# Two K loads of a grouped-query attention kernel, cut into a 96-row transfer and four 8-row transfers

## The chip, the cores and the metric

The kernel runs on one core of one Trainium2 chip. A core has five engines that matter here: TensorE (PE in the profile; its weight loads are the row PEld), VectorE (DVE), ScalarE (ACT), GpSimd (POOL) and SyncE (SP), which here does nothing but issue transfers. The transfers themselves are carried out by 16 DMA engines that belong to the core. The metric is the device time of one execution in microseconds (us); smaller is better. A measurement of this kernel is the median of a few executions.

## The reference

Sixteen batches, 32 query heads that share 8 key/value heads, 16 query positions, 2048 key positions, head size 128, all in bf16:

```python
B, Hq, Hkv, Sq, Sk, D = 16, 32, 8, 16, 2048, 128
k = jnp.repeat(k, Hq // Hkv, axis=1)
v = jnp.repeat(v, Hq // Hkv, axis=1)
scores = jnp.einsum("bhqd,bhkd->bhqk", q, k) * D ** -0.5
p = softmax(scores, axis=-1)
return jnp.einsum("bhqk,bhkd->bhqd", p, v)
```

K and V are 64 MiB each and are read once; q and the output are 2 MiB each. Four query heads of 16 positions share one K/V head, so each K/V head has 64 query rows.

## The kernel before, in words

The 128 K/V heads are taken in 64 pairs (index p, NP = 64) and the pairs in 32 groups of two (index Q, or n in the load function). One K load brings four heads: 2 MiB, as 128 partitions (rows) of 16 KiB that are contiguous in memory, into one of three buffers (`Kn`, NK = 3). One V load brings one pair: 1 MiB, each partition getting two runs of 4 KiB, into one of seven buffers (`Vb`, NV = 7). The last V load is cut in two along the key positions.

For each pair the steps are these. VectorE turns the K data around in 32x32 blocks (`kt`, L351, two instructions for each pair) into one of two buffers `KT`. TensorE forms the scores (S, L300 and L256). VectorE scales and negates them into SBUF, rearranged, and keeps the row minimum (L373). ScalarE takes the exponential with the row sum (L413). TensorE transposes the probabilities (PT, L312), ScalarE copies them out of PSUM (L423), TensorE multiplies them with V (PV, L330 and L336), and ScalarE, or VectorE for the last five pairs, scales the result by the reciprocal row sum (L436, L440, L394). GpSimd lays out the queries for the coming pairs (L174).

Every engine's program is written out by hand in a fixed order; semaphores tie the programs together. All transfers are issued by SP, in one order given by a loop over t: at an even t the K load t/2, then the V load of pair t-6, then the store of pair t-14, and every eighth step a load of q. SP issues them in that order and blocks at the first whose buffer is not free: a K load n waits until both transposes of both pairs of load n-3 are done (`sem_kt`), a V load until the product of pair p-7 is done (`sem_pv`), a store until its output tile is written.

Each transfer raises its semaphore by 16 in all, in sixteen increments of one. VectorE's wait for a K load stands ahead of the first transpose of a group and asks for all sixteen of each load that has used this buffer:

```python
if x == 0:
    dve.wait_ge(sem_k[Q % NK], 16 * (Q // NK + 1))
```

The change touches `load_k` in SP's program (L208) and this wait in `kt` in VectorE's program (the transposes are L351).

Of the kernel before, what the change touches and what calls it, by code (L numbers as in the profile page):

```python
# [11 lines left out]
NK = 3  # L12
# [11 lines left out]
LASTV = ((0, 12), (12, 16))  # L24
NFAST = 8
NLATE = 5


def both_heads(p, NP):
# [3 lines left out]
def bass_standalone__gqa_softmax__sampling_kernel(  # L33
# [28 lines left out]
    Kn = [sb(f"Kn{i}", [128, 4 * J * 128], BF16) for i in range(NK)]  # L62
# [19 lines left out]
    sem_k = [sem(f"sem_k{i}") for i in range(NK)]  # L82
# [19 lines left out]
    kf = k.rearrange("b h s d -> (b h s d)").rearrange("(n a x) -> n a x", n=NQD, a=128)  # L102
# [9 lines left out]
    def q_part(c, i):  # L112
        u = stage("Q", c, i)
        pe_prog.append(("QT", c, i, u))
        act_prog.append(("qe", c, i, u))

    def pv(p):
        pe_prog.append(("PV", p))
# [4 lines left out]
    def exp(p):  # L123
        act_prog.append(("exp", p))
# [11 lines left out]
    for p in range(NP - 2):  # L136
# [7 lines left out]
        if c + 1 < NQC and 2 <= i < 6:  # L144
            q_part(c + 1, i - 2)
    for p in range(NP - 2 - PVLAG, NP - NLATE):
        pv(p)
        norm(p)
    exp(NP - 2)
    exp(NP - 1)  # L150
    for p in range(NP - NLATE, NP - 3):
        pv(p)
# [11 lines left out]
    def o_ap(p):  # L164
        if p < NP - 4:
            return O_ps[:, 0:128]
        x = p - (NP - 4)
        return S_ps[:, 512 * x:512 * x + 128]

    def lay_q(eng, c):  # L170
        eng.wait_ge(sem_q[c % NQ], 16 * (c // NQ + 1))
        src = Qn[c % NQ][:, :, :].rearrange("p j (b x) -> p (j b) x", b=2)
        for r in range(4):
            eng.tensor_scalar(  # L174
                Q4[:, :, :, r, :].rearrange("p j b x -> p (j b) x"), src,
                mask[:, r:r + 1], None, op0=ALU.mult,
            ).then_inc(sem_q4, 1)

    with nc.Block() as block:

        @block.gpsimd
        def _(gp):
            gp.iota(iota_m[:, :, :], [[-8, 4], [-32, 4]], base=0, channel_multiplier=1).then_inc(sem_id, 1)
            gp.iota(iota_t[:, :], [[1, 128]], base=0, channel_multiplier=-1).then_inc(sem_id, 1)
            gp.wait_ge(sem_id, 2)
            gp.tensor_scalar(ident4[:, :], iota_t[:, :], 0.0, None, op0=ALU.is_equal).then_inc(sem_id, 1)
            gp.tensor_scalar(lo_m[:, :, :], iota_m[:, :, :], 0.0, None, op0=ALU.is_ge).then_inc(sem_id, 1)
            gp.tensor_scalar(hi_m[:, :, :], iota_m[:, :, :], 8.0, None, op0=ALU.is_lt).then_inc(sem_id, 1)
            gp.wait_ge(sem_id, 5)
            gp.tensor_tensor(lo_m[:, :, :], lo_m[:, :, :], hi_m[:, :, :], op=ALU.mult).then_inc(sem_id, 1)  # L190
            for x in range(2):
                gp.wait_ge(sem_id, 6 + x)
                a = lo_m[:, :, :] if x == 0 else hi_m[:, :, :]
                w = 2 >> x
                dst = hi_m[:, :, 0:2] if x == 0 else mask[:, :].unsqueeze(2)
                gp.tensor_tensor(dst, a[:, :, 0:w], a[:, :, w:2 * w], op=ALU.add).then_inc(sem_id, 1)
            gp.wait_ge(sem_id, 8)
            for c in range(1, NQC):
                gp.wait_ge(sem_st, last_q[c - 1, 3] + 1)
                lay_q(gp, c)  # L200

        @block.sync
        def _(sp):
            def load_k(n):
                s = n % NK
                if n >= NK:
                    sp.wait_ge(sem_kt, 4 * (n - NK) + 4)
                sp.dma_start(Kn[s][:, :], kf[n]).then_inc(sem_k[s], 16)  # L208

            def load_v(p):  # L210
                s = p % NV
                if p >= NV:
                    sp.wait_ge(sem_pv, p - NV + 1)
                if p < NP - 1:
                    dst = Vb[s][:, :, :, :].rearrange("a g j d -> a g (j d)")
                    sp.dma_start(dst, vf[:, 2 * p:2 * p + 2, :]).then_inc(sem_v[s], 16)
                    return
                for x, (lo, hi) in enumerate(LASTV):
                    dst = Vb[s][:, :, lo:hi, :].rearrange("a g j d -> a g (j d)")
                    src = vf[:, 2 * p:2 * p + 2, 128 * lo:128 * hi]  # L220
                    sp.dma_start(dst, src).then_inc(sem_vl[x], 16)

            def load_q(c):
                s = c % NQ
                if c >= NQ:
                    sp.wait_ge(sem_q4, 4 * (c - NQ + 1))
                src = qf[1024 * c:1024 * (c + 1), :].rearrange("(a j) d -> a j d", j=8)
                sp.dma_start(Qn[s][:, :, :], src).then_inc(sem_q[s], 16)

            def store(p):  # L230
                s = p % NO
                if p < NP - NLATE:
                    sp.wait_ge(sem_nm, p + 1)
                else:
                    sp.wait_ge(sem_nl, p - (NP - NLATE) + 1)
                sp.dma_start(of[128 * p:128 * (p + 1), :], Osb[s][:, :]).then_inc(sem_o[s], 16)

            for t in range(NP + SLAG + 1):
                for c in range(NQC):
                    if t == max(0, 8 * c - QLEAD):  # L240
                        load_q(c)
                if t < NP and t % 2 == 0:
                    load_k(t // 2)
                if 0 <= t - VLAG < NP:
                    load_v(t - VLAG)
                if 0 <= t - SLAG < NP:
                    store(t - SLAG)
            for s in range(NO):
                sp.wait_ge(sem_o[s], 16 * (NP // NO))
# [95 lines left out]
        @block.vector  # L345
        def _(dve):
            def kt(n, e):
                Q, x = divmod(n, 2)
                if x == 0:
                    dve.wait_ge(sem_k[Q % NK], 16 * (Q // NK + 1))  # L350
                dve.transpose(  # L351
                    KT[n % NKT][:, :].rearrange("p (t b g e a) -> p e g t b a", t=J // 4, b=2, g=4, e=2)[:, e],
                    Kn[Q % NK][:, :].bitcast(F32).rearrange(
                        "p (g x t e b c) -> p x e g t b c", g=4, x=2, e=2, b=2, c=32)[:, x, e],
                ).then_inc(sem_kt, 1)

            def recip(Q):
                dve.wait_ge(sem_exp, 2 * Q + 2)
                dve.reciprocal(rrec[:, 2 * Q:2 * Q + 2], rowsum[:, 2 * Q:2 * Q + 2]).then_inc(sem_rec, 1)  # L359

            dve.wait_ge(sem_id, 8)
            lay_q(dve, 0)
            for n in range(2):
                for e in range(2):
                    kt(n, e)
            for n in range(NP):
                Q, x = divmod(n, 2)
                dve.wait_ge(sem_s, n + 1)
                for y in range(2):
                    p = 2 * Q + y  # L370
                    if x == 0 and p >= NS:
                        dve.wait_ge(sem_exp, p - NS + 1)
                    dve.tensor_scalar(  # L373
                        Sneg[p % NS][:, 1024 * x:1024 * (x + 1)].rearrange("p (t a m) -> p t a m", t=4, m=8),
                        S_ps[:, 1024 * y:1024 * (y + 1)].rearrange("p (t m a) -> p t a m", t=4, m=8), -scale, None,
                        op0=ALU.mult, op1=ALU.min, accum_out=nhalf[:, x, p:p + 1],
                    ).then_inc(sem_max, 1)
                if x == 1:
                    dve.wait_ge(sem_max, 2 * n + 2)
                    pair = slice(2 * Q, 2 * Q + 2)  # L380
                    dve.tensor_tensor(nbias[:, pair], nhalf[:, 0, pair], nhalf[:, 1, pair], op=ALU.min).then_inc(sem_nb, 1)  # L381
                elif n >= 4:
                    recip(Q - 2)
                if n + 2 < NP:
                    for e in range(2):
                        kt(n + 2, e)
            recip(NQD - 2)
            for p in range(NP - NLATE, NP):
                if p == NP - 2:
                    recip(NQD - 1)  # L390
                dve.wait_ge(sem_rec, p // 2 + 1)
                dve.wait_ge(sem_o[p % NO], 16 * (p // NO))
                dve.wait_ge(sem_pv, p + 1)
                dve.tensor_scalar(Osb[p % NO][:, :], o_ap(p), rrec[:, p:p + 1], None, op0=ALU.mult).then_inc(sem_nl, 1)  # L394
# [75 lines left out]
```

## Time and profile before

| what | us |
|---|---|
| median of three executions | 342.99 |
| lowest and highest of them | 342.74, 343.7 |
| span of the profiled execution, first to last instruction | 340.7 |
| a time of the profiled execution beside its span | not recorded |
| median less that span | 2.3 |
| PE busy | 304.3 |
| DVE busy | 304.8 |
| ACT busy | 253.6 |
| POOL busy | 81.3 |
| DMA: mean rate, share of 16 engines' time on the transfer queue | 408 GB/s, 99.5% |
| 32 K loads of 2048 KB, median from issue to landing | 15.3 |
| 63 V loads of 1024 KB, median from issue to landing | 16.6 |

The first part of the profile's page gives busy time by engine over the whole span; the second cuts the span into 40 slices and gives each engine's busy share in tenths; the third gives the transfer queues, where q1 carries the kernel's own transfers and q8 and q14 carry instructions. The fourth follows the chain of work that ended last back from the end. The fifth and sixth group instructions and transfers by line. Beside the page, the trace holds the record of every transferred packet (start, duration, size, queue, but not the DMA engine) and the time of every increment of a load's semaphore; "landing" is the last of the sixteen.

### The profile page before, as it was taken

Reading aid. Unit: us, or ns where it says so; the run is one execution under the profiler, and the core shown is the slowest. Engines: PE = TensorE matmul, PEld = TensorE weight load, DVE = VectorE, ACT = ScalarE, POOL = GpSimd, SP = SyncE. Lnnn points to the kernel's source line nnn. Section 1 sums busy time; section 2 is a strip of 40 time slices with the busy share of each in tenths; the row PEclk is TensorE's granted clock in tenths of the full one; section 3 lists DMA queues with packets and bytes.
Section 4 is the critical chain, followed back from the end, with each engine's and each line's share of the span. In section 5 each row is a group of like instructions: output and inputs, shape, how many; then the busy total and the mean of one; then the engine's idle time right before and its main releaser. Section 6 shows DMA issues by size and latency. Waiting matters only on the chain.

```text
span 340.7 us, 7084 instructions
## 1 busy us (share of the span) xinstructions
PE 304.3 (89%) x3040; PEld 182.4 (54%) x2528; DVE 304.8 (89%) x457; ACT 253.6 (74%) x390; POOL 81.3 (24%) x40
## 2 busy tenths in 40 slices
PE   3466798999899998999989999999989999899987
PEld 3012355555655664566555556556645665555556
DVE  1879998999989997999989999899979999899952
ACT  3025776789777888778867897778887788678875
POOL 2840007500092004900075000920039000000000
PEclk9759999999999999999999999999999999999999
DMA  7999999999999999999999999999999999999993
GB/s 294 443 415 420 425 415 414 411 419 422 424 423 410 415 419 424 416 420 407 419 426 423 419 405 417 421 428 415 412 418 416 426 418 423 408 419 415 410 407 121
DMA packets 32688, 138.87 MB, mean 408 GB/s; under 512 B 10896, under 2 KB 11152, under 8 KB 28560
## 3 DMA queue, kind: packets, MB, share of 16 engines
q1 hardware_dynamic: 32656, 138.42, 99.5%
q8 instruction: 22, 0.36, 0.4%
q14 instruction: 10, 0.08, 0.1%
HBM read 136.31 MB, written 2.10 MB: 406 GB/s over the span
## 4 chain that ended last, share of the span: by engine, by line
PE 55%; DVE 28%; ACT 9%; issue 5%; DMA 2%; ACTq 0%; SPq 0%; DVEq 0%
PE O_ps L330 17%; DVE Sneg L373 17%; PE S_ps L300 14%; PE S_ps L256 12%; DVE KT L351 11%; PE ST_ps L312 8%; ACT P L413 4%; ACT QT L404 2%; DMA Kn<-in_k_dram 2%; PE ST_ps L278 2%; ACT PT L423 2%; ACT O L436 1%; PE S_ps L336 1%; PE O_ps L336 1%; DVE rrec L359 0%
## 5 line engine op out<-in xcount | busy, mean ns | idle before, releaser
L373 DVE TENSOR_SCALAR_CACHE_REDUCE Sneg<-S_ps 128x1024 f32<-128x1024 f32 x128 | 150.7, 1213 | 19.1 <-PE S_ps L256 18.9
L351 DVE STREAM_TRANSPOSE KT<-Kn 128x1024 f32<-128x1024 f32 x128 | 150.8, 1217 | 3.9 <-DMA Kn<-in_k_dram 3.9
L413 ACT ACTIVATE P<-Sneg,nbias 128x2048 bf16<-128x2048 f32 x64 | 128.2, 2004 | 16.1 <-DVE nbias L381 15.1
L300 PE MATMUL S_ps<-KT,QT 64*128 64x512 bf16 x512 | 103.5, 394 | 24.1 <-DVE Sneg L373 12.8
L174 POOL TENSOR_SCALAR Q<-Qn,mask 128x1024 bf16<-128x1024 bf16 x28 | 79.1, 2843 | 181.1 <-PE ST_ps L278 174.6
L256 PE MATMUL S_ps<-KT,QT 64*128 64x512 bf16 x512 | 103.1, 392 | 0.0
L330 PEld LDWEIGHTS O_ps<-Vb,PT 128*128 128x128 bf16 x672 | 62.4, 98 | 34.7 <-issue 28.0
L330 PE MATMUL O_ps<-Vb,PT 128*128 128x256 bf16 x672 | 80.7, 273 | 0.0
L423 ACT ACTIVATE PT<-ST_ps 128x512 f32<-128x512 f32 x128 | 69.3, 595 | 13.1 <-PE ST_ps L312 12.1
L300 PEld LDWEIGHTS S_ps<-KT,QT 64*128 64x128 bf16 x512 | 27.4, 94 | 93.7 <-issue 72.4
L312 PE MATMUL ST_ps<-ident,P 128*128 128x128 f32 x512 | 67.6, 275 | 4.1 <-ACT P L413 4.1
L436 ACT ACTIVATE O<-O_ps,rrec 64x128 bf16<-64x128 f32 x84 | 30.4, 362 | 46.2 <-PE O_ps L330 45.7
L312 PEld LDWEIGHTS ST_ps<-ident,P 128*128 128x128 f32 x512 | 56.9, 141 | 10.3 <-ACT P L413 7.8
L278 PE MATMUL ST_ps<-ident,Q 128*128 128x128 f32 x128 | 20.4, 291 | 5.2 <-DVE Q L174 5.2
L404 ACT ACTIVATE QT<-ST_ps 128x512 f32<-128x512 f32 x32 | 19.3, 604 | 5.1 <-PE ST_ps L278 5.1
L336 PEld LDWEIGHTS O_ps<-Vb,PT 128*64 128x64 bf16 x576 | 16.7, 110 | 11.5 <-issue 11.5
L336 PE MATMUL O_ps<-Vb,PT 128*64 128x128 bf16 x576 | 19.5, 221 | 0.6 <-ACT O L440 0.6
L278 PEld LDWEIGHTS ST_ps<-ident,Q 128*128 128x128 f32 x128 | 16.4, 152 | 5.2 <-issue 5.2
L413 ACT ACTIVATION_READ_ACCUMULATOR P<-Sneg,nbias 128x1 f32 x64 | 12.2, 191 | 0.0
L373 DVE DVE_READ_ACCUMULATOR Sneg<-S_ps 128x1 f32 x128 | 10.6, 83 | 0.0
L440 ACT ACTIVATE O<-O_ps,rrec 128x128 bf16<-128x128 f32 x17 | 6.0, 351 | 2.2 <-PE O_ps L336 2.2
L381 DVE TENSOR_TENSOR nbias<-nhalf 128x2 f32<-128x2 f32 x32 | 5.1, 160 | 1.1
(19 smaller groups left out, 20.1 us busy)
## 6 DMA issues: line engine op xcount, KB each, us to landing
Kn<-in_k_dram SPq DMA_DIRECT2D x32, 2048.0 KB, 15.3
Vb<-in_v_dram SPq DMA_DIRECT2D x63, 1024.0 KB, 16.6
Qn<-in_q_dram SPq DMA_DIRECT2D x8, 256.0 KB, 13.3
out_dram<-O SPq DMA_DIRECT2D x64, 32.0 KB, 16.1
Vb<-in_v_dram SPq DMA_DIRECT2D x1, 768.0 KB, 12.0
Vb<-in_v_dram SPq DMA_DIRECT2D x1, 256.0 KB, 12.3
```

The lines of the kernel that those rows point to most:

```text
L174: eng.tensor_scalar(Q4[:, :, :, r, :].rearrange("p j b x -> p (j b) x"), src, mask[:, r:r + 1], None, op0=ALU.mult,).then_inc(sem_q4, 1)
L256: return pe.add_instruction(mybir.InstMatmult(name=nc.get_next_instruction_name(), engine=mybir.EngineType.PE, ins=[pe.lower_ap(rhs), pe.l ...
L278: ins = pe.transpose(dst[:, 128 * j:128 * (j + 1)], src[:, 4 * x + j, b, :], ident4[:, :])
L300: ins = pe.matmul(s_ap, w, x, start=(acc == 0), stop=(acc == 3))
L312: ins = pe.transpose(dst[:, 128 * t:128 * (t + 1)], P[p % 2][:, 128 * x:128 * (x + 1)], ident4[:, :])
L330: ins = pe.matmul(O_ps[:, 0:256], pt[:, j // 2, j % 2, :], Vb[p % NV][:, :, j, :], start=(j == 0), stop=(j == J - 1),)
L336: ins = pe.matmul(o_ap(p)[64 * g:64 * (g + 1), :], pt[:, j // 2, j % 2, 64 * g:64 * (g + 1)], Vb[p % NV][:, g, j, :], start=(j == 0), stop ...
L351: dve.transpose(KT[n % NKT][:, :].rearrange("p (t b g e a) -> p e g t b a", t=J // 4, b=2, g=4, e=2)[:, e], Kn[Q % NK][:, :].bitcast(F32). ...
L373: dve.tensor_scalar(Sneg[p % NS][:, 1024 * x:1024 * (x + 1)].rearrange("p (t a m) -> p t a m", t=4, m=8), S_ps[:, 1024 * y:1024 * (y + 1)] ...
L413: act.activation(P[p % 2][:, :].bitcast(BF16), Sneg[p % NS][:, :], ACT.Exp, bias=nbias[:, p:p + 1], scale=-1.0, accum_out=rowsum[:, p:p + ...
L423: act.activation(PT[p % NPT][:, 4 * h:4 * (h + 1), :].rearrange("p t q -> p (t q)"), stage_ap(u), ACT.Copy,).then_inc(sem_ev, 1)
L436: ins = act.activation(Osb[p % NO][rows, :], O_ps[rows, 128 * g:128 * (g + 1)], ACT.Copy, scale=rrec[rows, p:p + 1])
```

## The change

Two of the 32 K loads, number 14 and number 22, are issued as five transfers instead of one. First come four transfers of eight partitions each: partitions 96, 100, ..., 124, then 97, 101, ..., 125, then 98, ..., 126, then 99, ..., 127. The fifth brings partitions 0 to 95. Together they bring the same 128 rows of 16 KiB into the same buffer. Each of the five adds 16 to the buffer's semaphore, so VectorE's wait counts 80 for a cut load and 16 for any other that has used this buffer. Nothing else changes.

```diff
+KCUT = (14, 22)
+KROWS = 96
...
                 if n >= NK:
                     sp.wait_ge(sem_kt, 4 * (n - NK) + 4)
-                sp.dma_start(Kn[s][:, :], kf[n]).then_inc(sem_k[s], 16)
+                if n not in KCUT:
+                    sp.dma_start(Kn[s][:, :], kf[n]).then_inc(sem_k[s], 16)
+                    return
+                for a in range(KROWS, KROWS + 4):
+                    sp.dma_start(Kn[s][a::4, :], kf[n, a::4]).then_inc(sem_k[s], 16)
+                sp.dma_start(Kn[s][:KROWS, :], kf[n, :KROWS]).then_inc(sem_k[s], 16)
...
                 if x == 0:
-                    dve.wait_ge(sem_k[Q % NK], 16 * (Q // NK + 1))
+                    dve.wait_ge(sem_k[Q % NK], sum(80 if m in KCUT else 16 for m in range(Q % NK, Q + 1, NK)))
```

## The prediction

> **What bounds the kernel now.** I read the page first (busy shares, the slices, the transfer queues), then the waits, then the chain that ended last, and then the K loads one by one.
>
> ```profile
> PE 304.3 (89%) x3040; PEld 182.4 (54%) x2528; DVE 304.8 (89%) x457; ACT 253.6 (74%) x390; POOL 81.3 (24%) x40
> DMA  7999999999999999999999999999999999999993
> DMA packets 32688, 138.87 MB, mean 408 GB/s; under 512 B 10896, under 2 KB 11152, under 8 KB 28560
> q1 hardware_dynamic: 32656, 138.42, 99.5%
> q8 instruction: 22, 0.36, 0.4%
> q14 instruction: 10, 0.08, 0.1%
> PE 55%; DVE 28%; ACT 9%; issue 5%; DMA 2%; ACTq 0%; SPq 0%; DVEq 0%
> ```
>
> Two things run at their limit together: the 16 DMA engines are busy from the first slice to the last but one, and DVE and PE at 89%. The chain belongs to PE and DVE, with DMA 2%. So no transfer is waited for after the first, which the list of waits says too:
>
> ```profile
> DVE KT L351 <- DMA Kn<-in_k_dram: 3.9, 1, 3.9
> SPq L208 <- DVE KT L351: 123.5, 24, 10.5
> ```
>
> The only wait of DVE for K is at the start. SP waits 123.5 us for buffers: transfers are queued far ahead. How far is seen by load: 7.8 us from issue to landing at the least, 20.2 at the most. The answers for K28, K31 and for DVE's use of K31 (the window from 315.9) are
>
> ```profile
> L208 SPq DMA_DIRECT2D Kn<-in_k_dram x1: 328/328/328, 264.8 to 264.8; - x1
> DMA to landing us min/median/max: 20.2/20.2/20.2
> ...
> L208 SPq DMA_DIRECT2D Kn<-in_k_dram x1: 1220/1220/1220, 295.8 to 295.8; - x1
> DMA to landing us min/median/max: 19.9/19.9/19.9
> ...
> L351 DVE STREAM_TRANSPOSE KT<-Kn x2: 1201/1212/1222, 316.2 to 317.4; 128x1024 f32<-128x1024 f32 x2
> ```
>
> K31 is issued at 295.76, lands 19.85 later at 315.61 and is transposed from 316.24: a margin of 0.62 us. Done for all loads by the trace's increments and DVE's starts, the margin is 13.7 us at K3, 8.8 at K14, 8.1 at K15, 4.7 at K22, 4.0 at K23, 3.4 at K26, 2.6 at K27, 1.06 at K28, 2.3 at K29, 1.55 at K30, 0.62 at K31. It falls because DMA is the slower of the two: from K14 to K15 loads land 10.14 us apart, while eight pairs (four loads) take the chain 39.8 us (its PV pieces at 124.39 and 164.21). The last V load's two parts are issued at 324.03 and 324.5 and land 12.0 and 12.3 later, about 1.2 us before PE needs them. From 295 to 325.6 DVE runs without a gap in the chain. So an earlier landing gains nothing in this execution, and a later one costs all that goes beyond 0.6 us at K31 or 1.06 at K28.
>
> The sixteen increments of one load say how unequal the DMA engines are. In K4 they all come within 0.57 us. In K31 they come, from the first, at 0, 0.09, 0.33, 0.41, 0.51, 0.91, 2.77, 2.95, 3.07, 3.17, 3.28, 3.34, 3.76, 4.35, 4.39 and 4.58 us; in K28 at 0, 0.04, 0.28, 0.33, 0.44, 0.82, 2.80, 2.81, 2.86, 2.91, 2.94, 3.00, 3.02, 3.13, 3.29, 3.34. One increment jumps by about 1.5 us after each of the 16 KiB packets of q8 (the first starts at 41.7 us and takes 1.11): an instruction fetch delays the one DMA engine that it falls on, and as none is ever idle the lag stays until the end. Six are hardly touched, ten are late. A load lands when the latest has.
>
> **The change part by part.** Profiled execution: span 340.7, some 2.3 below the median of 342.99; I add the difference below to the median and take what lies around the span as unchanged.
>
> *Rows moved.* 32,688 packets less 28,560 under 8 KB leaves 4,128: the 4,096 rows of 16 KiB of K and 32 of the two instruction queues. So a row is one packet, never cut, and an 8-row transfer can occupy at most eight DMA engines, a 128-row one gives each of 16 eight rows, a 96-row one six. If the four small transfers go to the same eight, these get 4 + 6 = 10 rows of a cut load and the others 6. A row of K takes 0.611 us (median of the 4,096 packets, 608 to 1,586 ns between its ends, the latter in the cold first load). Two rows more in each of two loads: 4 x 0.611 = 2.44 us more on eight engines, 2.44 less on the other eight. Four more closing increments of 9 ns in each load add 0.07. Bounds: 0, if the four transfers alternate between two sets of eight; 36.7, if all 32 rows of a cut load went to one engine (38 rows in place of 8, 30 x 0.611 in each of two loads). I take 2.44, nearest to the row we have: every 128-row load splits evenly. The upper end would give 379 us and stays outside the range with the chance that I leave there.
>
> [...] No trace here shows an 8-row transfer, nor which of the engines are the late ones.
>
> *What of that is felt.* At K14 and K22 themselves the margins of 8.8 and 4.7 cover 1.22 and 2.44. The lag stays, though. At K28, if the eight that get more are the eight least late (up to 2.81), the landing moves from 3.34 to 2.81 + 2.44 = 5.25: 1.91 later, 0.85 beyond the margin. If the latest is among them, 2.44 - 1.06 = 1.38. At K31, best case 2.95 + 2.44 = 5.39 against 4.58: 0.81 later, 0.19 beyond the margin; worst 2.44 - 0.62 = 1.82. A shift at K28 makes DVE late and gives K31 as much margin back, so they don't add: +0.85 in the best case, +1.82 in the worst. Nine times in ten, eight drawn of sixteen hold one of the three latest of K31 (4.35 and more), which gives +1.6 to +1.8. Ten are late and only six early, so no choice of eight avoids a late one. The last V load (lag 4.9, margin 1.2) asks for less than K31. I take +1.6, toward the worst.
>
> *The wait.* VectorE's wait counts to 80 instead of 16. One semaphore wait as before, nothing else behind it; 0. It asks for five transfers where one was asked for, and the last of them lands as above. Behind it on DVE stand the transposes of two pairs, and behind these PE's scores, up to now covered by K14's and K22's margins.
>
> *SP.* Eight more issues. A K issue takes 0.33 us, a V issue 0.44 (0.33 to 5.5 when it is held up). 4 x 0.33 = 1.3 us in each cut load, before the 96 rows and the V load, store and q load behind them. Landing is 14.2 us after issue at K14 and 18.3 at K22, all of it queue, so the engines don't run dry: 0. Were that cover gone, 1.3 us would be waited for at each. Below: nothing is saved, as no issue is removed.
>
> *Bytes.* The same; 0. Rows stay contiguous pieces of 16 KiB, and every fourth row of memory is read by each small transfer, close to each other in time.
>
> Sum: 342.99 + 1.6 = 344.6, own range +0.85 to +1.82, so 343.8 to 344.8.
>
> **The rivals.**
>
> *Two writers for the same partitions' memory.* Today partitions 96 to 127 are written by the engines that always write them, each row at 27.2 GB/s (from 4 KiB packets of 0.159 us and 16 KiB of 0.611: 12,288 B in 0.452 us). With the change other engines write them while their usual writers write theirs. If the way into a group of partitions carries only what one engine does, both run at half rate during the four rows: 4 x 0.611 = 2.44 more for both, per load. Then the eight lag 2 x (1.22 + 2.44) = 7.3, and at K31 7.3 - 0.62 = 6.7: 349.7; if the 96 rows are split so that two engines meet as well, more. For it: slope and size of the packets allow a limit at either end. Against: no packet after the first loads shows such a slowdown, but there is no case of two in this trace either. [...] Chance 0.26.
>
> *Hidden, or not done.* The small transfers alternate over the engines, or timed executions have more margin at K28 and K31 than the profiled one: 343.0. Against it: the profile's margin of 0.62 is what the trace shows. Chance 0.14.
>
> *SP held up.* Some issues take 2.8 us (K25) and up to 5.5. Four at 2.8 are 11.2 us, against K22's margin of 4.7: 6.5 felt, 349.5. It decides only when the queue of 18.3 us has run out. Chance 0.06.
>
> *Faster.* The engines that get more rows are the six early ones and two whose lag is there only in the profile. Then the eight stand at 0.91 + 2.44 = 3.35 at most, the others at 4.58 - 2.44, and K31 lands 4.58 - 3.35 = 1.2 earlier. The time falls by what executions wait for loads there, at most 1.2: 341.8. It decides only if the timed executions wait more than 1 us for K, where the profiled one waits for none after the first. Chance 0.06.
>
> **How the numbers follow.** A measurement of this kernel can tell 0.3%, 1.03 us. The forecast has 0.48, of which 0.10 lies under +1.03. Faster: 0.06. Within 0.3%: 0.14 + 0.10 = 0.24. Slower: 0.38 + 0.26 + 0.06 = 0.70. The range goes from 342.8, below the hidden case, to 349.8, above the two at 349.5 and 349.7; outside lie the faster case and the larger prices of two writers.
>
> **What would show it.** Right: 16 KiB packets of K14 and K22 still 0.61 us; the increments after K14 moved by 1.22 us up for eight and down for eight, twice that after K22; waits of DVE on Kn of 1 to 2 us in all, at K28 to K31; SP's issues of 0.33. Two writers: packets of 1.2 us at K14 and K22. Hidden: no wait of DVE on Kn after the first. Wrong altogether: a spread of the increments at K31 that is smaller than 4.58, or DVE and PE groups that change in busy time.

## The result, and the profile after

The changed kernel takes 361.82 us (median of four executions, 360.73 to 361.99) against 342.87 for the kernel before in the same comparison (341.87 to 343.7): a ratio of 1.0555, 95% interval 1.0534 to 1.0576. It is 19 us slower, where 1.6 had been forecast, and outside the range given (342.8 to 349.8). The sign was right, the size was not.

The page of the changed kernel: its span, the DMA rows of the forty slices (8.97 us each here), and the chain by engine and line.

```profile
span 358.9 us, 7092 instructions
DMA  8999999999999999999999999999999999999992
GB/s 317 431 410 420 417 423 423 415 412 410 423 418 429 422 348 223 380 420 411 414 420 419 421 423 315 210 253 420 415 418 421 417 419 417 418 419 418 393 389 87
PE 44%; DMA 21%; DVE 21%; ACT 7%; issue 4%; SPq 3%; ACTq 0%; DVEq 0%
DMA Kn<-in_k_dram 21%; PE O_ps L337 14%; DVE Sneg L380 12%; PE S_ps L307 11%; PE S_ps L263 10%; DVE KT L358 8%; PE ST_ps L319 6%; ACT P L420 3%; ACT QT L411 2%; SPq L223 1%; PE ST_ps L285 1%; ACT O L443 1%; ACT PT L430 1%; PE S_ps L343 1%; PE O_ps L343 1%
```

The same rate in the kernel before, in slices of 8.52 us:

```profile
GB/s 294 443 415 420 425 415 414 411 419 422 424 423 410 415 419 424 416 420 407 419 426 423 419 405 417 421 428 415 412 418 416 426 418 423 408 419 415 410 407 121
```

Two holes stand in the GB/s row of the changed kernel, in its 15th to 17th and 25th to 27th slice: there the rate falls from about 420 to 223 and 210 GB/s. The DMA row above it shows no hole: the DMA engines are as busy as ever (99.3% of their time on the transfer queue, 99.5 before). They move half as much in the same busy time. The chain, which had 2% of DMA, now has 21%, all of it on K loads.

The waits and the K rows of the changed kernel, first DVE's total wait for K with its count and its longest, then the issues with their durations in ns (lowest, median, highest):

```profile
DVE KT L358 <- DMA Kn<-in_k_dram: 20.2, 6, 12.1
...
L211 SPq DMA_DIRECT2D Kn<-in_k_dram x30: 327/432/2211, 1.2 to 314.5; - x30
L214 SPq DMA_DIRECT2D Kn<-in_k_dram x8: 623/623/1288, 125.3 to 213.1; - x8
L215 SPq DMA_DIRECT2D Kn<-in_k_dram x2: 438/438/438, 128.1 to 213.8; - x2
```

DVE waited 3.9 us for K before; now it is 20.2, one wait alone 12.1. The two holes by windows (the last two columns are the share of the DMA engines' time and GB/s), before:

```profile
132.00:142.00 10.00, 8.53 (x97) 4.82 (x79) 8.51 (x13) 7.92 (x13) 9.28 (x4) 1.00 1.01 415
220.00:240.00 20.00, 19.50 (x214) 12.01 (x180) 19.76 (x30) 16.48 (x25) 3.66 (x2) 1.00 1.03 420
```

and after:

```profile
132.00:142.00 10.00, 8.79 (x101) 5.25 (x83) 8.47 (x13) 7.90 (x12) 8.54 (x4) 1.00 1.03 223
220.00:240.00 20.00, 12.86 (x132) 7.71 (x108) 9.43 (x14) 11.64 (x18) 4.85 (x2) 0.96 1.03 222
```

In the first window compute does the same as before (DVE 8.51 and 8.47): K14's margin of 8.8 us covers it. In the second, DVE falls from 19.76 to 9.43. The packet records say what halved the rate: from 132.0 to 145.5 us and from 219.75 to 240.75 nearly every packet in flight, 14 to 18 of them at a time, takes about twice its time (a K row 1.17 us in place of 0.611, a V row 0.32 in place of 0.159). Outside the two stretches hardly a packet is slow (51 of the K and V rows after the first 20 us take over 1.3 times the usual). Added up over the packets and divided by 16 engines, the loss is 6.7 us in the first stretch and 10.4 in the second. Landings follow: K15 lands 7.6 us later than before (156.47 against 148.91), K23 19.3 later, K31 18.7 later. Less the margin of 0.62 at K31 that is 18.1; the span has grown by 18.2.

The increments of K14's semaphore also show how an 8-row transfer is carried out: there are 52 for the five transfers, 16 for the 96 rows and nine for each small one. Four come 0.00, 0.72, 1.39 and 2.06 us after the first of them, at SP's four issues; the other 48 from 6.2 us on. The page counts 64 packets under 512 B more than before (10,960 against 10,896), eight for each of the eight small transfers, where a load of 128 rows has sixteen increments, as many as there are DMA engines. Read so, eight engines take part in a small transfer with an increment each; 48 of the 80 that the wait asks for come this way, and the four at SP's issues bring the other 32, eight each.

### The profile page after: what moved, and what is told of

Read it like the earlier page. It is cut to its first block, busy times and chain, and to the rows that moved or that the text cites. A ratio compares the mean times of both kernels' runs of the same rounds, so it can differ in the third digit from the quotient of the medians.

```text
span 358.9 us, 7092 instructions
## 1 busy us (share of the span) xinstructions
PE 307.8 (86%) x3040; PEld 183.4 (51%) x2528; DVE 305.5 (85%) x457; ACT 254.0 (71%) x390; POOL 81.4 (23%) x40
## 2 busy tenths in 40 slices
DMA packets 32752, 138.87 MB, mean 387 GB/s; under 512 B 10960, under 2 KB 11216, under 8 KB 28624
## 3 DMA queue, kind: packets, MB, share of 16 engines
q1 hardware_dynamic: 32720, 138.42, 99.3%
## 4 chain that ended last, share of the span: by engine, by line
PE 44%; DMA 21%; DVE 21%; ACT 7%; issue 4%; SPq 3%; ACTq 0%; DVEq 0%
DMA Kn<-in_k_dram 21%; PE O_ps L337 14%; DVE Sneg L380 12%; PE S_ps L307 11%; PE S_ps L263 10%; DVE KT L358 8%; PE ST_ps L319 6%; ACT P L420 3%; ACT QT L411 2%; SPq L223 1%; PE ST_ps L285 1%; ACT O L443 1%; ACT PT L430 1%; PE S_ps L343 1%; PE O_ps L343 1%
## 5 line engine op out<-in xcount | busy, mean ns | idle before, releaser
L358 DVE STREAM_TRANSPOSE KT<-Kn 128x1024 f32<-128x1024 f32 x128 | 150.9, 1218 | 20.2 <-DMA Kn<-in_k_dram 20.2
L307 PE MATMUL S_ps<-KT,QT 64*128 64x512 bf16 x512 | 105.2, 400 | 38.8 <-DVE Sneg L380 27.7
L263 PE MATMUL S_ps<-KT,QT 64*128 64x512 bf16 x512 | 104.8, 397 | 0.0
L411 ACT ACTIVATE QT<-ST_ps 128x512 f32<-128x512 f32 x32 | 19.3, 603 | 5.1 <-PE ST_ps L285 5.1
## 6 DMA issues: line engine op xcount, KB each, us to landing
Kn<-in_k_dram SPq DMA_DIRECT2D x30, 2048.0 KB, 18.9
```

What stands on the lines that cost most here:

```text
L263: return pe.add_instruction(mybir.InstMatmult(name=nc.get_next_instruction_name(), engine=mybir.EngineType.PE, ins=[pe.lower_ap(rhs), pe.l ...
L307: ins = pe.matmul(s_ap, w, x, start=(acc == 0), stop=(acc == 3))
L358: dve.transpose(KT[n % NKT][:, :].rearrange("p (t b g e a) -> p e g t b a", t=J // 4, b=2, g=4, e=2)[:, e], Kn[Q % NK][:, :].bitcast(F32). ...
```

## The experiments

What was known by now: rows take twice their time while a cut load is under way. The theory, A: when two DMA engines write into partitions of the same group, they share what one can carry, so the rival of the prediction, but with the 96 rows at fault as well. No trace names the engine of a packet, so which engines write which partitions is an assumption of this theory throughout. Its rivals: B, only the four small transfers do it; C, only the lag of the extra rows; and a fourth, the mere number of transfers, issues and increments.

**The parts by themselves.** A kernel of loads only, one kind after the other on an idle queue (the helpers, one for each kind, are left out here):

```diff
+plan = [(rows_128, 1), (rows_96, 1), (rows_128, 1), (rows_64, 1), (rows_32, 1),
+        (small_high, 4), (small_low, 4), (small_next, 4), (five, 5), (rows_96, 1), (five, 5)]
+for n, (what, c) in enumerate(plan):
+    what(n, sems[n])
+    done(sems[n], c)
```

> This kernel computes nothing: it only issues loads of K rows on an idle queue, each waiting for the one before, and stores the last. Order: 128 rows, rows 0 to 95, 128 rows, rows 0 to 63, rows 96 to 127, the four small transfers of the change, the same four on partitions 0 to 31 (every fourth), four of eight neighbouring rows, all five of the change, rows 0 to 95 again, all five again. Theory A (two DMA engines that write rows of the same group of partitions share one engine's rate, and the 96 rows are dealt out six to an engine without regard to who usually writes them): packets of 0.61 us in the 128 rows, of 1.2 us in the 96, 64 and 32 rows, 0.61 in both four-apart sets (each set of eight rows has one writer per group when it is alone), up to 2.4 in neighbouring rows; the five together are slower than the 96 rows and the four small ones are alone. Theory B (only the small transfers are at fault): the 96 rows alone have packets of 0.61 and land in 6/8 of the time of 128. Theory C (no sharing, only the extra lag that was predicted): packets of 0.61 throughout, the five land 2 x 0.61 = 1.2 us later than the 128 rows.

Its transfers by size, with the median from issue to landing in us:

```profile
A<-in_k_dram SPq DMA_DIRECT2D x4, 1536.0 KB, 9.1
A<-in_k_dram SPq DMA_DIRECT2D x2, 2048.0 KB, 7.8
A<-in_k_dram SPq DMA_DIRECT2D x1, 1024.0 KB, 7.3
A<-in_k_dram SPq DMA_DIRECT2D x1, 512.0 KB, 4.4
```

96 rows take longer than 128 (9.1 against 7.8), and 64 rows nearly as long (7.3). The packets agree: a median of 0.611 us in the 128 rows, 1.08 in the 96, 1.27 in the 64, 1.08 in the 32. The four small transfers alone have medians of 0.79 (96 to 127) and 0.69 (0 to 31), 41% of them at 0.61, though theory A had written 0.61 for both; four of neighbouring rows, 2.09. All five of the change land 13.6 and 14.0 us after the first issue, some 6.1 more than one load of 128. B and C fall: 96 rows are slow with nobody else there (1.08 us a row).

**Three ways to cut the same two loads.** Without small transfers; with the small ones on partitions 0 to 31; and along the row, in five transfers of the same bytes:

```diff
 # two_parts
+sp.dma_start(Kn[s][KROWS:, :], kf[n, KROWS:]).then_inc(sem_k[s], 16)
 sp.dma_start(Kn[s][:KROWS, :], kf[n, :KROWS]).then_inc(sem_k[s], 16)
 # low_rows
+for a in range(4):
+    sp.dma_start(Kn[s][a:32:4, :], kf[n, a:32:4]).then_inc(sem_k[s], 16)
+sp.dma_start(Kn[s][32:, :], kf[n, 32:]).then_inc(sem_k[s], 16)
 # columns
+for a in range(4):
+    x = slice(512 * a, 512 * (a + 1))
+    sp.dma_start(Kn[s][:, x], kf[n][:, x]).then_inc(sem_k[s], 16)
+sp.dma_start(Kn[s][:, 2048:], kf[n][:, 2048:]).then_inc(sem_k[s], 16)
```

> Both loads in two transfers, rows 96 to 127 in one and rows 0 to 95 in the other, so no 8-row transfer and no engine with more rows than another. Theory A: the 96 rows still meet, so most of the 18.9 us stays: 355 to 365 us. Theory B (the small transfers are at fault): 343 to 345. Theory C (lag by extra rows): 343.

> [...] Theory A: the 96 rows still meet: 352 to 362 us. Theory B: the small transfers now write where they always did, so only the lag is left: 343.5 to 345. Theory C: as the change without sharing, 344.6, which the change itself has already missed.

> The same two loads in five transfers with the same bytes in each, but cut along the row: four of 128 rows of 1 KiB and one of 128 rows of 12 KiB. [...] Theories A, B and C: no meeting and no lag, 342.5 to 343.5 us. A fourth theory (the number of transfers, SP's issues or the wait for five increments is at fault): about 362.

Against before (343.0): two parts 358.37, ratio 1.0426 (1.0375 to 1.0477); small ones on the low rows 358.7, 1.0475 (1.0416 to 1.0534); columns 342.9, 1.0002 (0.9988 to 1.0016). The slices of the two-part kernel:

```profile
GB/s 315 424 417 421 417 428 414 417 413 412 421 421 424 424 346 201 365 416 413 415 421 420 422 422 360 192 267 419 421 421 420 422 419 415 414 417 420 409 400 98
```

and of the columns:

```profile
GB/s 289 441 417 420 425 418 411 409 420 425 419 417 418 411 422 410 424 410 413 419 422 432 412 408 417 410 425 422 408 419 415 430 412 425 409 419 416 410 406 120
```

Cutting a load in five along the row costs nothing. Cutting it into 96 and 32 rows costs 15 of the 19 us, with no 8-row transfer in sight. So the number of issues, the wait for 80 increments and the bytes are cleared, as the prediction had them at 0.

**One cut at a time.**

```diff
-KCUT = (14, 22)
+KCUT = (14,)   # only14;  (22,) only22;  (4,) only4
```

> Only load 14 is cut, as the change cuts it. In the changed kernel's trace loads land 7.6 us later from K15 on and 19.3 later from K23 on. If each cut costs what its own meeting of writers costs, whatever went before: 7.6 less the margin of 0.62 at K31, 350 us. If the two cost the same and the trace's split is chance: 9.5 less 0.6, 352. If the lag alone did it (predicted): 343 to 344.

> Only load 22 is cut. If the second cut costs more because the engines are further apart by then through their own fetches of instructions: 11.7 less 0.6, 354 us. If it costs more because the first cut has spread them: about 350, as with load 14. The sum of this and the run with load 14 alone, counted from before, should come to 18.9 plus 0.6 if the cuts are independent.

Load 14 alone: 349.74 against 342.54, ratio 1.0203 (1.0180 to 1.0226), 7.2 us. Load 22 alone: 350.85, 1.0241 (1.0221 to 1.0261), 8.3; of the two figures written for it, "about 350" holds. Together 15.5, less than the 19 of both. Each run alone has K31's margin of 0.6 taken off, both together only once, so independent cuts would add up to 0.6 less than 19 (the expectation adds the 0.6 where it has to be taken off). The 2.8 us that are missing then say that a second cut is dearer after a first. Counted from the packets (quarters of a us in which most of those in flight take over 1.3 times the usual), the time at half rate is 14.0 us with load 14 alone, 16.5 with load 22 alone, and 13.5 and 21.25 in the changed kernel. What differs ahead of them is how far the sixteen engines have come apart: the increments of the load before the cut come within 2.2, 3.4, 2.1 and 6.2 us. That it is the spread was read from the runs afterwards; load 4, where the spread is smallest, puts it to a test:

> Only load 4 is cut, where the DMA engines are still in step: in the trace of before the sixteen increments of K4 come within 0.6 us, those of K13 within 2.0 and those of K21 within 3.3. Load 14 alone cost 2.03%, load 22 alone 2.41%. If the half rate lasts as long as any engine still has a row to write in another's partitions, and so longer the further apart the engines are: 5.5 to 6.5 us, what the five cost in a stretch without compute (6.5 to 7.4 there) less the margin, 348.2 to 349.2. If the cost is the same wherever the cut is: 349.7 to 351. If an early cut is made up for, as its margin of 13 us is large: 343 to 345.

346.75 against 342.92, ratio 1.0108 (1.0076 to 1.0140): 3.8 us. The direction is as the theory says, but none of the three ranges written holds: 346.75 lies below 348.2. The 6.5 to 7.4 us that it was taken from (the five between whole loads without compute, below) were a poor measure. The time at half rate is 10.75 us at a spread of about 0.6 (K3, 0.8 in this execution). Its slices fall to 291 and 295 GB/s, not to 223 and 210:

```profile
GB/s 304 442 411 291 295 419 418 426 420 412 413 417 422 427 413 419 409 421 419 427 420 413 416 415 421 423 427 409 412 419 423 424 421 412 419 415 418 411 409 129
```

So 10.75, 14.0, 16.5 and 21.25 us of half rate stand beside spreads of 0.8, 2.2, 3.4 and 6.2: about 1.9 us more for each us of spread (10.5 over 5.4). Counted in the same way, the kernel with two parts has 13.75 and 17.25 us at spreads of 1.9 and 3.5, a little above this line. The kernel with the low rows has 13.75 and 16.25 us at 2.0 and 5.1, and for the last of these the line gives 18.9. So with the same cut the half rate lasts longer where the engines are further apart, but that the spread is what lengthens it is not shown. An early cut is not made up for by a margin of 13 us: the DMA engines' share is 1.01 and 1.02 in the windows from 26 to 38 and from 40 to 50 us, with no pause in which to catch up, and K31 lands 4.4 us late (320.03 against 315.61).

**Extra rows, with all loads whole.** Here nothing is cut. Four times, four transfers of eight rows of 7 KiB are loaded in addition into a tile that nobody reads. Only the partitions differ: 0 to 31, 96 to 127, 32 to 63 and 4 to 35, in the order of the expectations.

```diff
+if n in (14, 17, 20, 23):
+    ...  # wait until the extra rows of the batch before have landed
+    for a in range(P0, P0 + 4):
+        sp.dma_start(Xt[a:P0 + 32:4, :], kf[n, a:P0 + 32:4, 0:3584]).then_inc(sem_x, 16)
 sp.dma_start(Kn[s][:, :], kf[n]).then_inc(sem_k[s], 16)
```

> All loads uncut. In addition, ahead of loads 14, 17, 20 and 23, four transfers each of eight rows of 7 KiB (partitions 0, 4, ..., 28 and so on) into a tile that nobody reads: bytes that the kernel before does not move. [...] So eight engines get 16 rows of about 0.27 us more, 4.35 us of lag, and nobody meets. By the prediction's step on what a lag costs: 2.8 us (the eight least late get it; from K28: 2.81 + 4.35 - 3.34 - 1.06) to 3.7 (the latest are among them; from K31: 4.35 - 0.62), so 345.8 to 346.7. If a lag is made up for somewhere: 343 to 344.

> [...] No 96-row transfer. Theory A (two writers of a group of partitions share one engine's rate): both are slowed while they meet, so 4.35 us come on top for the eight and as much for their partners: 348 to 351. If the small transfers' place does not matter and the 96 rows did all of it: as with partitions 0 to 31, 345.8 to 346.7.

> The extra 7 KiB rows go to partitions 32 to 63. If what counts is who writes a group of partitions in the uncut loads, and partitions 32 to 63 belong to the same eight engines as 0 to 31 in the same order, this is the run with partitions 0 to 31 over again: 345.5 to 346.5. If any place but 0 to 31 meets: 350 to 356.

> [...] If the meeting is between an engine and the usual writer of the partitions, the same eight engines now carry the lag, the slower foreign rows and the slower own rows: 4.35 + 4.35 + 4.35 at a fair share, 13 less 0.6, so 355, and up to 364 at double that price. If only partitions 64 to 127 make trouble: 345.5 to 346.5.

| partitions | us | before | ratio (95%) |
|---|---|---|---|
| 0 to 31 | 345.9 | 342.54 | 1.0094 (1.0075 to 1.0113) |
| 32 to 63 | 346.16 | 342.93 | 1.0095 (1.0070 to 1.0120) |
| 96 to 127 | 354.99 | 342.54 | 1.0361 (1.0336 to 1.0385) |
| 4 to 35 | 355.25 | 342.93 | 1.0358 (1.0317 to 1.0400) |

The first two cost what a pure lag would: 3.4 and 3.2 us for an estimated 4.35 us of rows on eight engines, inside the 2.8 to 3.7 that the prediction's step gives. Partitions 32 to 63 behave as 0 to 31 (346.16 and 345.9 us; DVE's waits for K are 7.9 and 7.3 us, against 17.1 with 96 to 127 and 16.3 with 4 to 35). The last two rows cost 9 us more for the same bytes, again through eight engines for each transfer (144 increments for sixteen transfers). The run with 96 to 127 lies above both ranges written for it (348 to 351 at most). Shifting by four partitions is enough (1.0358 against 1.0094). All four runs read their rows with the same step in memory, so the reading does not make the difference; where the rows are written does. The author's reading, with the same eight engines in all four runs, is that what matters is whether an engine writes into partitions that another engine writes in the whole loads; as no trace names the engine, that is not shown.

How the rate falls, in the window from 132 to 136 us around the first of the four batches, with the rows in partitions 0 to 31:

```profile
132.00:136.00 4.00, 2.79 (x25) 1.16 (x15) 2.63 (x5) 3.94 (x7) 2.96 (x2) 1.00 1.04 437
```

with the rows in 96 to 127:

```profile
132.00:136.00 4.00, 2.79 (x25) 1.25 (x17) 2.51 (x3) 3.18 (x5) 3.88 (x2) 1.00 1.05 256
```

and in 4 to 35:

```profile
132.00:136.00 4.00, 2.79 (x25) 1.17 (x15) 2.64 (x5) 3.94 (x7) 2.96 (x2) 1.00 1.03 251
```

This is where theory A in its first form falls. In the runs with 0 to 31 and 32 to 63 no such stretch is seen, so by the theory these partitions, and with them 4 to 35, belong to the eight engines that carry the extra rows. If only writers of the same partitions slowed each other, the same eight engines with shifted rows would slow themselves only. But in both slow cases nearly every packet in flight is slow between about 132 and 135.5 us, 14 to 18 of them at a time, and the earliest increment of K14 moves as well (137.07 us with the rows in 0 to 31, 138.87 shifted, 138.66 in 96 to 127): even the first increment of the sixteen is 1.6 to 1.8 us late. The loss over all packets is some 34 us of engine time in each batch, about 2.1 us for each of sixteen engines and 8.5 in the four batches, which is nearly the 9 us.

**A meeting by itself.** Two whole loads, something in the middle, two whole loads, without compute:

```diff
+plan = [none, low, high, rows_96, five] * 2
+for i, what in enumerate(plan):
+    ...
+    c = whole(n, 0, s) + whole(n, 1, s)
+    c += what(n, s)
+    c += whole(n, 2, s) + whole(n, 3, s)
+    sp.wait_ge(s, 16 * c)
```

> This kernel computes nothing. Ten stretches, each waiting for the one before: two whole K loads, something in the middle, two whole K loads, all into tiles of their own. In the middle: nothing; the four small transfers on partitions 0 to 31; the same on 96 to 127; rows 0 to 95; all five of the change. Then all five kinds again. From the first issue to the last landing, against nothing in the middle: partitions 0 to 31, 4 rows of 0.61 more on eight engines, 2.4 us. Partitions 96 to 127: 2.4 + 2.4 = 4.9 if two writers share fairly while they meet; some 6 to 7 if a meeting costs about twice that, as the run with the extra rows in these partitions suggests. Rows 0 to 95: 3.7 if nobody met (six rows for each engine), 7 if each row meets another. All five, which is one more load of 128 rows: 4.9 if nobody met, 6.1 with the lag of two rows, 11 to 16 with meetings.

From the first issue to the last landing, from the trace's increments (us, both rounds):

| in the middle | time | more than nothing |
|---|---|---|
| nothing | 22.46, 22.51 | |
| small ones, partitions 0 to 31 | 24.44, 24.40 | 1.9 |
| small ones, 96 to 127 | 27.07, 27.02 | 4.6 |
| rows 0 to 95 | 30.07, 29.58 | 7.3 |
| all five | 34.81, 33.91 | 11.9 |

With the small ones on 0 to 31, eight increments of the last load stay where they were (21.8 to 22.3) and eight come 1.9 later: lag and nothing else. With 96 to 127 the first eight come at 24.6 and the others at 27.0: all sixteen lose 2.6 us. The 96 rows would take 3.7 with rows at 0.611 and take 7.3, twice that. The five are 128 rows, 4.9 us as a whole load (8 x 0.611); they cost 7.4 and 6.5 more than that. This is close to the 7.6 by which loads after K14 land late. How the 96 rows are dealt out to the engines is not known, on the reading side either, so for them reading and writing are not told apart; for the small transfers the runs with extra rows do that.

## Why the prediction was wrong, point by point

*What bounds the kernel* held. The margins of 8.8 at K14 and 0.62 at K31 carried over: the first hole leaves DVE as busy as before, and K31's 18.7 less 0.62 is the growth of the span. The second cut found its margin used up by the first (DVE already waits 0.8 to 1.5 us at each of K19 to K21), so DVE waited 12.1 us at K22.

*Rows moved* is the step that failed. Its count of engines was right (nine increments for each small transfer, one of them at SP's issue, are read as eight engines, sixteen for the 96 rows as all). Its 2.44 also needs the same eight engines each time, which no trace shows directly; in the meeting by itself, four small transfers on partitions 0 to 31 make eight increments 1.9 us late and leave the other eight in place, as it would be with the same eight. But then it gave every row the 0.611 us of an uncut load, 2.44 us in all. In the cut loads a row takes 1.17 us, and so does nearly every other K row meanwhile. The term is 6.7 and 10.4 us for all sixteen engines, in place of 2.44 for eight.

*What of that is felt* was right for the lag, where it can be seen alone: 3.2 to 3.4 us measured, 2.8 to 3.7 by the same working. Of the 19 us it is a small part. Its lower bounds rest on a misreading: the increments given for K28 are those of K27. K28's own end at 4.39 us, so an eighth engine at 2.80 + 2.44 = 5.24 lands 0.85 later, inside the margin of 1.06 there, and the best case is K31's +0.19 in place of +0.85; for the extra rows K31 gives 2.1 in place of 2.8. The +1.6 and the top of the range, which come from K31, stand.

*The wait* and *bytes*, at 0, held: five transfers along the row give a ratio of 1.0002. So does *SP*, though a small transfer's issue takes 0.62 us and not 0.33.

*The rival "two writers for the same partitions' memory"* is the nearest to what happened, with 0.26 of the chance and the wrong price. Its sign, packets of 1.2 us at K14 and K22, was seen at 1.17. It had two engines share for the duration of the four small rows: 6.7 us, 349.7. That other engines than before write partitions 96 to 127 was its assumption, which no trace shows. Two things were missing. The 96 rows slow the others as well, which the text set aside as "more", outside the range; with the 32 rows in one transfer in place of the small ones, the ratio is still 1.0426 of 1.0555. And the slowing takes in all sixteen engines (all sixteen increments lose 2.6 us in the meeting by itself, with the small ones on 96 to 127), which the two-engine picture has no term for. "Hidden" and "faster" are refuted by the 19 us and by DVE's waits. "SP held up" is refuted by the columns and by the issues themselves: the eight of 0.62 to 1.29 us never let the DMA row drop.

The choice behind the miss: with no case of two writers in the trace, the price of a row was taken from the nearest row, the uncut load, though that row differed in the one thing that the change touched, how a load's rows are dealt out to transfers. The rival's doubled time for a row, applied to the 128 rows of all engines instead of to four rows, would have been 4.9 us for each load, and 352 in all: still half of the growth. Why the stretches at half rate are longer than that stays open.

## What to carry to other kernels

If a load of all 128 partitions must be cut, cut it along the row and not by partitions: here, with two loads of 32, the one cost nothing (1.0002) and the other 4 to 6% (1.0426 to 1.0555). Loads cut into 96 and 32 rows brought the rate of everything in flight from about 420 GB/s to 201 and 192 in the lowest slices, and four transfers of eight rows into partitions 4 to 35 or 96 to 127 brought it to 251 and 256. As the DMA engines were busy for 99.5% of the time already in the kernel before, the price was the whole queue's time and not that of the cut load's own bytes. Transfers of 64 and 32 rows were slow alone (1.27 and 1.08 us a row, against 0.611 in 128); what they do to others was not measured by itself. The lag from the cut of load 4 stayed to the end (K31 landed 4.4 us late), and the margin of 13 us at the place of the change was no cover for it.

## What the runs showed of the hardware that was not expected

Four 8-row transfers into partitions 4 to 35 or 96 to 127 slowed nearly every packet in flight, 14 to 18 at a time: the rate was 251 and 256 GB/s, where the same transfers into 0 to 31 left it at 437, and K14's first increment came 1.8 and 1.6 us later. In the meeting by itself all sixteen increments lost 2.6 us to small transfers into 96 to 127, against those into 0 to 31. Alone on an idle queue, the small transfers into partitions 96 to 127 are little slower than those into 0 to 31 (medians of 0.79 and 0.69 us a row). Why all the packets in flight are drawn in, and how exactly the 96 rows are dealt out to the engines, stays open: the packet records don't name the engine.

One load of 96 rows takes longer than one of 128 (9.1 us against 7.8). And the same cut costs 3.8 us at load 4, 7.2 at load 14 and 8.3 at load 22: the later the load, the further the engines have come apart before it and the longer the half rate lasts.
